# Sliding-window attention as banded matmuls on an even/odd token order, with the row sums as a 29th column of V

## The chip, the cores and the metric

One core of one Trainium2 chip (trn2). The metric is device time in microseconds (us) of one execution; lower is better. A run of a kernel here means several executions, and the median is quoted. Medians are over all executions; ratios are over fast ones alone. Some executions are marked slow: one of four in qk_twice, rz_merge and cap4_merge_flex, two of six in cap4_flex_zg. All other runs quoted are in the fast state.

Engines are named as the profile names them: PE (TensorE matmuls), PEld (its weight loads), DVE (VectorE), ACT (ScalarE), POOL (GpSimd), SP (the queue that issues DMAs). PEclk is the TensorE clock that was granted, as a share of full speed.

## The reference, cut to what matters

One transformer block on 2048 tokens of width 448: a sliding-window attention (A) and a token-shift MLP (B), with residuals.

```python
def _A_ref(x, wqkv, wo):                # H = 16 heads of 28, W = 8, dil = 2
    q, k, v = split(x @ wqkv)
    idx = pos[:, None] - off[None, :]   # off = 0, 2, 4, ..., 14: eight keys per query
    logits = einsum("bhsd,bhswd->bhsw", q, k[idx]) * 28 ** -0.5   # masked where idx < 0
    o = einsum("bhsw,bhswd->bhsd", softmax(logits), v[idx])
    return o @ wo
def _B_ref(x, w1, w2, w3, w4):
    h = gelu(layernorm(x) @ w1)         # then four column groups shifted by +1, -1, +2, -2 tokens
    x1 = x + shifted(h) @ w2
    return x1 + gelu(layernorm(x1) @ w3) @ w4
h = x + _A_ref(layernorm(x), ...)
out = h + _B_ref(layernorm(h), ...)
```

Each query reads only eight keys, all of its own parity (even or odd token).

## The kernel before

The program is written as a list of operations with a small list scheduler that orders each engine's instructions. Tokens go in four tiles of 512. The attention of one tile, shortened:

```python
# A2: products q*k for all eight offsets on DVE, summed over the head dimension by PE
for c in range(4):
    dve("tensor_tensor", out=ring(slot), in0=q_broadcast, in1=k_shifted, op=mult)   # 112 x 4096
for c in range(4):
    for a8 in range(8):
        mm(L, zc[:, c, 7 - a8 : 7 - a8 + 128], ring(slot)[:, a8*512:(a8+1)*512])     # indicator weights
# softmax over w: DVE max, subtract; ACT exp; DVE sum, reciprocal, multiply
dma(Pd, pb)                       # probabilities to DRAM ...
dma(ring(slot), Pd, broadcast)    # ... and back, copied to the 28 partitions of each head
# A3: products p*v on DVE, summed over the window by identity matmuls on PE
for c in range(4):
    dve("tensor_tensor", out=r4, in0=r4, in1=v_shifted, op=mult)                     # 112 x 4096
for c in range(4):
    for w in range(8):
        mm(ps[0:112, b, :], ident[0:112, 0:112], r4[:, :, w, :], w == 0, w == 7)
    act(actT, ps, Copy)
# then WO, with a further identity matmul that adds the residual xin
```

LayerNorm takes its inverse square root by three Newton steps on DVE, and its normalization runs on ACT. PSUM banks are handed out in a fixed rotation.

## Time and profile before

306.95 us (306.94 to 307.39, three executions).

| | us |
|---|---|
| span of the profiled execution | 306.6 |
| PE busy | 260.6 (85%) |
| DVE busy | 168.8 (55%) |
| ACT busy | 154.7 (50%) |
| PE not busy (306.6 - 260.6) | 46.0 |

From the page of before, parts 1 and 2: first busy time, share of the span and instructions of each engine; then the span in 40 equal slices, each digit the busy share in tenths.

```profile
PE 260.6 (85%) x1297; PEld 136.4 (44%) x1297; DVE 168.8 (55%) x346; ACT 154.7 (50%) x240; POOL 19.7 (6%) x44
...
PE   0499959959995799996777988949899999989996
...
DVE  3659889983799728985762789001801640200221
...
PEclk9999979979999599998999999986999999999999
```

The left half (attention) has both PE and DVE full and empty in turn; the right half (MLP) is PE, with little else. The same by stretches, cut at 144 us (columns: stretch, its length, busy time of PE, PEld, DVE, ACT, POOL with instruction counts, granted clock, DMA share, GB/s):

```profile
0.00:144.00 144.00, 115.18 (x530) 62.37 (x531) 109.46 (x183) 65.09 (x102) 3.58 (x28) 0.95 0.53 126
144.00:306.60 162.60, 145.41 (x768) 74.07 (x766) 59.32 (x164) 89.57 (x138) 16.08 (x16) 0.97 0.16 41
```

Much of the PE work on the left is arithmetic that a matmul of q with k would not need. Groups of instructions by shape (the line L630 is a helper's that issues everything, so groups are told apart by their names: name of output and inputs, stationary and moving shape, count | busy us in total, mean ns of one | idle time before them and who ended it):

```profile
L630 DVE TENSOR_TENSOR arena<-arena 112x4096 bf16<-112x4096 bf16 x32 | 72.0, 2287 | 17.6 <-PE ps L630 9.5 <-DMA arena<-attn_p_scratch 7.5 <-ACT arena L630 0.3
L630 PE MATMUL ps<-actT,arena 112*112 112x512 bf16 x192 | 51.0, 432 | 13.3 <-ACT actT L630 12.7 <-DVE arena L630 0.7
L630 PE MATMUL ps<-arena,ident 112*112 112x512 bf16 x128 | 28.8, 380 | 0.8 <-DVE arena L630 0.8
L630 PE MATMUL ps<-arena,zc 112*128 112x512 bf16 x128 | 28.3, 380 | 0.0
```

These are the two rounds of DVE products, QKV, the identity matmuls that sum over the window, and the indicator matmuls that sum over the head dimension. The chain of waits (start us, length us, what) shows how they alternate for one tile:

```profile
101.60 14.55 PE ps L630 x56
116.18 13.30 DVE arena L630 x6
```

### The profile page before, as it was taken

To read this page: it belongs to the slowest core of one execution; us is meant where nothing else is said; L and a number is where in the kernel's file an instruction comes from. 1 tells how busy PE (TensorE), PEld (TensorE's weight loads), DVE (VectorE), ACT (ScalarE), POOL (GpSimd) and SP (SyncE) were. 2 spreads that over 40 slices of the span, in tenths; PEclk is the share of its full clock that TensorE was granted. 3 is DMA by queue.
4 is the path that set the end of the run, shared out by engine and by line. 5 is a ranking of instruction groups with operands and counts; after the bars stand their busy time and mean duration, and the time that the engine had idled before them with its cause. 6 is when DMAs were issued, how large, how long until landed. Compare 5 with 4: busy or idle time off the path is not lost.

```text
span 306.6 us, 3389 instructions
## 1 busy us (share of the span) xinstructions
PE 260.6 (85%) x1297; PEld 136.4 (44%) x1297; DVE 168.8 (55%) x346; ACT 154.7 (50%) x240; POOL 19.7 (6%) x44
## 2 busy tenths in 40 slices
PE   0499959959995799996777988949899999989996
PEld 0254435526542365452444554425445544544552
DVE  3659889983799728985762789001801640200221
ACT  1522346446730567524897568695663167066000
POOL 4000000000000000000000005002205002300000
PEclk9999979979999599998999999986999999999999
DMA  7900018837850299915885000000000100100111
GB/s 224 327 4 0 3 32 202 197 84 175 195 112 0 63 200 207 205 33 145 196 178 191 0 0 2 0 1 0 2 0 30 33 0 0 47 15 0 32 45 45
DMA packets 11824, 24.71 MB, mean 81 GB/s; under 512 B 1376, under 2 KB 9120, under 8 KB 10016
## 3 DMA queue, kind: packets, MB, share of 16 engines
q1 hardware_dynamic: 11808, 24.50, 32.6%
q8 instruction: 10, 0.16, 0.2%
q14 instruction: 6, 0.05, 0.1%
HBM read 22.13 MB, written 2.36 MB: 80 GB/s over the span
## 4 chain that ended last, share of the span: by engine, by line
PE 53%; DVE 27%; ACT 15%; issue 3%; DMA 1%
PE ps L630 53%; DVE arena L630 17%; ACT actT L630 7%; ACT lntm L630 4%; ACT arena L630 3%; DVE st L630 3%; DVE rs_t L630 1%; DVE rs_y L630 1%; DMA xin<-in_A_x_dram 1%; DVE mv L630 1%; DVE ls L630 1%; ACT ls L630 1%; DVE mx L630 1%; ACT L630 0%; DVE rs_x L630 0%
## 5 line engine op out<-in xcount | busy, mean ns | idle before, releaser
L630 PE MATMUL ps<-actT,arena 112*128 112x512 bf16 (+1 forms) x416 | 100.8, 404 | 17.2 <-ACT actT L630 16.6
L630 ACT ACTIVATE arena<-ps 112x512 bf16<-112x512 f32 (+1 forms) x114 | 68.0, 597 | 46.4 <-PE ps L630 46.3
L630 DVE TENSOR_TENSOR arena<-arena 112x4096 bf16<-112x4096 bf16 x32 | 72.0, 2287 | 17.6 <-PE ps L630 9.5
L630 PEld LDWEIGHTS ps<-actT,arena 112*128 112x128 bf16 (+1 forms) x416 | 48.7, 121 | 66.7 <-ACT actT L630 22.2
L630 ACT ACTIVATE actT<-ps 112x1024 bf16<-112x1024 bf16 (+1 forms) x40 | 32.6, 846 | 29.5 <-PE ps L630 29.5
L630 DVE TENSOR_TENSOR ost<-ps,arena 128x448 bf16<-128x448 f32 x16 | 10.0, 625 | 64.6 <-PE ps L630 64.6
L630 PE MATMUL ps<-arena 128*128 128x448 bf16 x224 | 42.9, 353 | 0.0
L630 ACT ACTIVATE lntm<-xin,nbias,rs_y 128x448 bf16<-128x448 bf16 x32 | 22.9, 750 | 17.6 <-DVE nbias L630 17.6
L630 PEld LDWEIGHTS ps<-arena 128*128 128x128 bf16 x224 | 21.9, 98 | 20.7
L630 PE MATMUL ps<-arena,ident 112*112 112x512 bf16 x128 | 28.8, 380 | 0.8 <-DVE arena L630 0.8
L630 PE MATMUL ps<-arena,zc 112*128 112x512 bf16 x128 | 28.3, 380 | 0.0
L630 DVE BATCH_NORM_STATS2 st<-xin 128x6 f32<-128x448 bf16 x32 | 19.3, 604 | 15.6 <-ACT xin L630 11.0
L630 PE MATMUL ps<-ident,lntm 128*112 128x128 bf16 x192 | 15.5, 229 | 13.9 <-ACT lntm L630 13.8
L630 POOL TENSOR_TENSOR arena<-arena,xin 128x448 f32<-128x448 f32 x16 | 16.1, 1035 | 110.8 <-ACT lntm L630 110.8
L630 PE MATMUL ps<-wo_s,actT 112*128 112x448 bf16 x64 | 17.2, 379 | 6.7 <-ACT actT L630 6.4
L630 PE MATMUL ps<-actT,w_s 112*112 112x512 bf16 x64 | 18.6, 441 | 4.6 <-ACT actT L630 4.6
L630 PEld LDWEIGHTS ps<-arena,ident 112*112 112x112 bf16 x128 | 16.5, 130 | 11.9 <-DVE arena L630 1.3
L630 PEld LDWEIGHTS ps<-ident,lntm 128*112 128x112 bf16 x192 | 14.0, 136 | 17.2 <-ACT lntm L630 15.0
L630 DVE TENSOR_TENSOR arena<-ps,arena 128x448 f32<-128x448 f32 x16 | 9.6, 599 | 21.7 <-PE ps L630 21.6
L630 PEld LDWEIGHTS ps<-arena,zc 112*128 112x128 bf16 x128 | 12.4, 98 | 15.0 <-issue 0.2
L630 ACT ACTIVATE ls<-ls 128x512 f32<-128x512 f32 x4 | 2.5, 630 | 28.4 <-DVE ls L630 28.4
L630 PEld LDWEIGHTS ps<-actT,w_s 112*112 112x112 bf16 x64 | 9.0, 150 | 12.2 <-ACT actT L630 6.6
(39 smaller groups left out, 134.4 us busy)
## 6 DMA issues: line engine op xcount, KB each, us to landing
arena<-attn_p_scratch SPq DMA_DIRECT2D x64, 224.0 KB
arena<-in_B_w_dram SPq DMA_DIRECT2D x2, 1568.0 KB, 11.5
xin<-in_A_x_dram SPq DMA_DIRECT2D x4, 448.0 KB, 8.2
out_dram<-ost SPq DMA_DIRECT2D x16, 112.0 KB, 1.7
arena<-in_A_wqkv_dram SPq DMA_DIRECT2D x1, 1176.0 KB, 7.4
w_s<-in_B_w_dram SPq DMA_DIRECT2D x2, 392.0 KB, 8.8
attn_p_scratch<-pb SPq DMA_DIRECT2D x4, 128.0 KB, 1.8
wo_s<-in_A_wo_dram SPq DMA_DIRECT2D x1, 392.0 KB, 10.3
```

Of the source, the lines that this page charges most:

```text
L630: inst = getattr(eng, op.meth)(**op.kw)
```

## The change

The intent is to let PE do both products. Tokens are kept in even and odd halves, so the eight keys of a query are eight neighbours, and 103 queries of one parity need 110 consecutive keys. One matmul of 110 keys by 103 queries (28 deep) then makes a whole band block for a head; exp runs on ACT without a maximum, a 0/1 mask on DVE cuts the block to its band, and a second matmul multiplies by V. V has a 29th column that is constant, so its product is the row sum times that constant. The row sums lie in one partition per head and are packed by DMA over 128 partitions for the reciprocal, stored, and broadcast back.

```diff
+    BLK = [(103 * b, 103, 103 * b + 1) for b in range(4)] + [(412, 100, 410)]   # query start, count, key start
+    KB = 110
@@ attention of one tile (t = token half and parity)
+        for c in range(4):                       # four heads per c
+            for jp in range(2):
+                T = tile(2)                      # two PSUM banks
+                for q0, nq, k0 in BLK:
+                    for j in (2 * jp, 2 * jp + 1):
+                        mm(T[0:KB, j % 2, q0:q0 + nq], kT[32*j:32*j+28, par, c, k0:k0 + KB],
+                           qT[32*j:32*j+28, par, c, q0:q0 + nq], True, True)
+                act(pj, T, ACT.Exp, 1024, scale=SCALE)
+                dve("tensor_tensor", 1024, out=pj, in0=pj, in1=m_, op=ALU.mult)
+            T = tile()
+            for blk, (q0, nq, _) in enumerate(BLK):
+                for j in range(4):
+                    mm(T[32*j:32*j+32, 0, q0:q0 + nq], vt[0:KB, par, blk, 4*c + j, :], pt[0:KB, sl, j, q0:q0 + nq], True, True)
+            copy(osb[:, par, c, :], T)
+        for j in range(4):
+            dma(zp[32*j:32*j+32, par, :], osb[32*j+28:32*j+29, par, :, :])       # pack the row sums
+        dve("reciprocal", out=rzp[:, par, :], in_=zp[:, par, :])
+        dma(zd, rzp[:, par, :])
+        for j in range(4):
+            dma(rzb[32*j:32*j+32], bass.AP(rz_d, (4*t + j) * 2048, [[0, 32], [1, 2048]]))   # broadcast
+        for c in range(4):
+            dve("tensor_tensor", out=oT[:, par, c, :], in0=osb[:, par, c, :], in1=rzb[:, c, :], op=ALU.mult)
... (cuts: loads, LayerNorm, MLP phases)
@@ LayerNorm: power on POOL, normalization on DVE (ACT before)
+        S.add("pool", "tensor_tensor", ..., in0=vtmp, in1=mhalf, op=ALU.pow)
+        S.add("dve", "tensor_scalar", 390, ..., op0=ALU.subtract, op1=ALU.mult)
@@ WO: the residual is added by DVE from PSUM, no identity matmul
+            dve("scalar_tensor_tensor", ..., in0=T, scalar=DOWN, in1=xin, op0=ALU.mult, op1=ALU.add)
@@ scheduler: PSUM banks chosen while ordering; a copy may go to ACT or DVE; shorter look-ahead
+        for b in range(0, 8, n): ...             # place(n): first free run of n banks
@@ end: exp without a maximum can overflow, so the old program stays as a second path
+                        emit_fast(e, eng)
+                        eng.wait_ge(flag_op.sem, flag_op.val)
+                            eng.reg_load(reg, flag[0:1, 0:1])
+                            with eng.If_ne(reg, 0):
+                                emit_general(e, eng)
```

## The prediction

> **What bounds the kernel now.** The page's busy table gives PE 260.6 of 306.6 us, DVE 168.8, ACT 154.7. Split at 144 us (busy by stretches): attention holds 115 us of PE and 109 us of DVE work in 144 us; the MLP part holds 145 us of PE in 163 us and is PE-bound. Attention alternates: in the chain of waits, DVE products (13.3 us for six 4096-wide multiplies, twice), then max/subtract/exp, then PE bursts of 54 to 56 matmuls. Much of that PE work is overhead: groups by shape show 28.3 us of 128 matmuls that sum products over the head dimension, 28.8 us of 128 identity matmuls that sum over the window, 6.1 us of 16 identity matmuls for the residual.
>
> **Removed.** PE: 28.3 + 28.8 + 6.1 = 63 us. DVE: 32 multiplies at 2287 ns (72 us), max/subtract/sum/divide (about 12 us), the Newton chains (about 25 us, now a power on POOL). ACT: 64 normalizations (45 us, now on DVE), the residual copy (8.5 us). 3.6 MB of broadcast DMA per 512 tokens becomes 1 MB.
>
> **Added.** PE: 640 attention matmuls of about 103 columns. The nearest thing in the trace is a transpose of 128 columns: 16 run in 1.05 us, weight loads hidden, about 55 ns each apart from the first. Estimate 45 to 50 ns, so about 30 us. The Trainium skill (TensorE: Matmul & The Clock Gate, Part 3) says that matmuls in different 32-row groups run concurrently, which could make it 22; TensorEngine Tiling (Key Properties) says that changing the tiling mode drains the array, which costs some back. No run shows either yet. QKV: 128 matmuls with 128 weight columns at 222 ns instead of 266, plus 80 of 448 columns: 45 us against 51.
> ACT: 32 exponentials of 110x1024, about 1.02 us each by the 1024-wide copy, 33 us. DVE: 32 mask multiplies near 0.65 us (21 us), 16 output scalings at 0.69 us (11 us), 64 normalizations near 0.35 us. Copies out of PSUM go to ACT or DVE.
> Row sums: gather, reciprocal, store, broadcast: three DMA legs near 2 us, about 10 us of latency per tile, hidden where other tiles' matmuls fill it.
>
> **Sum.** PE: 260.6 - 63 - 6 + 30 = about 221 us. In attention ACT and DVE hold about 72 us each against 92 of PE, so PE bounds it if the order overlaps well. PE idle: 12 until the first dense matmul (now 14.9; the padded weight copy waits for the weights); 12 in attention; 6 in the MLP part (17 now); 4 at the end, with the flag test and the branch over the general path; 4 for lower clock. Total 221 + 38 = 259 us.
>
> Predicted 259 us, 8 in 10 between 246 and 274. Faster by over 2%: 0.97; within 2%: 0.02; slower: 0.01.
>
> **What would show it.** PE busy 215 to 230 us and 80% or more of the span; DVE and ACT 110 to 150 each; the 640 small matmuls at 25 to 35 us in the groups; last attention matmuls before 125 us; PE never waiting over 3 us for the reciprocal's broadcast; the last 130 us a near solid PE row.
>
> **What would make it wrong.** Small matmuls at 80 ns or more (weight loads exposed): +20 us. Half clock in attention. Mask multiplies not at the 4096-wide rate: +17 us of DVE. Exp or PSUM banks holding up PE: attention becomes ACT-bound. The last tile's reciprocal chain exposed: +5 to 10. Row groups overlapping fully: about 8 us less.

## The result, and the profile after

251.51 us (249.73 to 252.7, four executions) against 307.06 us in the same rounds: ratio 0.8183, 95% interval 0.8144 to 0.8221. Ratios here are the mean time of fast runs of one kernel over that of the other (in the experiments the profiled execution itself is left out), so they are not quite the quotient of the medians. The predicted 259 (246 to 274) holds the measured time. A second run (after_again, chip 14) gave 252.39 us, ratio 0.8223.

The page after, the same parts:

```profile
PE 224.6 (90%) x1681; PEld 112.9 (45%) x1681; DVE 138.2 (55%) x306; ACT 120.7 (48%) x175; POOL 46.2 (18%) x71
...
PE   0799799999979998898995999899998999899992
...
DVE  7596862595785677877999602700385008700220
...
PEclk9999659999965995589998899999999999999998
```

PE busy falls by 36.0 us (260.6 to 224.6) and PE not busy by 20.0 us (46.0 to 26.0); together that is the whole 56.0 us between the two profiled spans. By stretches, cut at 115 us:

```profile
0.00:115.00 115.00, 99.26 (x1012) 53.07 (x1013) 81.23 (x185) 72.99 (x100) 20.30 (x41) 0.85 0.42 97
115.00:250.60 135.60, 125.35 (x671) 59.83 (x669) 56.94 (x122) 47.68 (x75) 25.90 (x31) 0.98 0.08 22
```

The first stretch is no longer shared between PE and DVE in turn: PE is busy for 99.26 of 115 us. But its clock is 0.85, lower than the 0.95 of before. The groups by shape name what came, and what the clock did:

```profile
L1100 PE MATMUL ps<-hT,arena 112*128 112x512 bf16 x128 | 39.4, 453 | 0.5 <-ACT hT L1100 0.2 <-ACT arena L1100 0.2
L1100 ACT ACTIVATE pt<-ps 110x1024 bf16<-110x1024 f32 x32 | 30.3, 1030 | 7.8 <-PE ps L1100 7.8
L1100 DVE TENSOR_TENSOR pt<-pt,msk 110x1024 bf16<-110x1024 bf16 x32 | 21.0, 684 | 1.7 <-ACT pt L1100 1.7
L1100 PE MATMUL ps<-qT,kT 28*110 28x103 bf16 x256 | 11.8, 232 | 3.8 <-ACT pt L1100 3.5
L1100 PE MATMUL ps<-pt,vt 110*32 110x103 bf16 x256 | 8.0, 253 | 2.0 <-DVE pt L1100 1.4 <-ACT pt L1100 0.7
L1100 PE MATMUL ps<-qT,kT 28*110 28x100 bf16 x64 | 6.5, 220 | 0.0
L1100 PE MATMUL ps<-pt,vt 110*32 110x100 bf16 x64 | 4.3, 253 | 0.0
```

The last four lines are the 640 small matmuls, each kind in two shapes. Their busy times must not be added (11.8 + 8.0 + 6.5 + 4.3 = 30.6 us): the last two matmuls of a burst, of the other shape, run while the earlier ones still do, and the overlap would count twice. The page, which puts the shapes together, has for the scores:

```profile
L1100 PE MATMUL ps<-qT,kT 28*110 28x103 bf16 (+1 forms) x320 | 13.2, 229 | 3.8 <-ACT pt L1100 3.5
```

With 9.1 us for the products with V, put together in the same way, the 640 small matmuls are busy for 22.3 us. The exponentials and the masks cost what the copies and the products of before implied. The surprise is the first line: 128 projections of q and k, which at the 222 ns each of the same shape in before should take 28.4 us, take 39.4 us. The line of before:

```profile
L630 PE MATMUL ps<-actT,arena 112*128 112x512 bf16 x224 | 49.7, 380 | 3.9 <-ACT actT L630 3.9
```

Why, can be seen where the small matmuls run alone. The order of PE in one such place (start us, length us, instruction, count, idle time before it and who ended it):

```profile
66.82 1.24 PE L1100 MATMUL ps<-qT,kT 28*110 28x103 bf16 x40
68.39 0.46 PE L1100 MATMUL ps<-qT,kT 28*110 28x103 bf16 x10 [0.33 <-ACT pt L1100]
69.30 0.46 PE L1100 MATMUL ps<-qT,kT 28*110 28x103 bf16 x10 [0.46 <-ACT pt L1100]
70.22 0.46 PE L1100 MATMUL ps<-qT,kT 28*110 28x103 bf16 x10 [0.46 <-ACT pt L1100]
```

The first 40 are four groups of two banks each: with that all eight PSUM banks hold scores that wait for their exponential. From there PE gets one bank pair back per exponential (one in 0.91 us), fills it with ten matmuls, and waits; no projection can start, as it has no bank (cap4, below, tests this). The ten take 0.46 us, of which the last one's own length is 0.21 us: in the trace's records they start in pairs 3 ns apart, one pair every 51 ns after the first, so the array is fed for only about a quarter of a microsecond in 0.91. The Trainium skill (TensorE: Matmul & The Clock Gate, Part 3) gives about 4 ns between the starts of matmuls in different row groups; 3 ns agrees.

Then the clock falls. Busy time by stretches of 3 us (columns as above; the clock is the third number from the end):

```profile
24.00:27.00 3.00, 1.55 (x40) 1.05 (x34) 2.96 (x9) 3.00 (x5) 0.00 (x0) 0.92 1.05 220
27.00:30.00 3.00, 2.56 (x33) 1.33 (x34) 2.73 (x7) 2.67 (x4) 1.54 (x2) 0.50 1.09 325
30.00:33.00 3.00, 3.00 (x16) 0.97 (x14) 2.39 (x4) 1.01 (x1) 0.61 (x1) 0.50 0.41 133
33.00:36.00 3.00, 3.00 (x45) 1.21 (x45) 0.94 (x2) 1.51 (x2) 0.00 (x0) 0.50 0.02 5
```

ACT is full (3.00 of 3) in the first line, PE half empty. In the following lines PE is nearly or quite full again (2.56, then 3.00 of 3), but it runs at half clock. The trace's clock records put this spell at 26.5 to 36.7 us; there are further ones at 70.9 (10.2 us), 94.8 (13.7 us) and 135.7 (3.4 us), 37.5 us in all before the last store, against 23.9 us in before, though before has 56 us more span. In the records of after, the q and k projections start 426 ns apart (median) at half clock and 216 ns apart at full clock, so up to half of such a spell is lost if PE is full in it.

### The profile page after: what moved, and what is told of

It is laid out like the page before. It is cut to its first block, busy times and chain, and to the rows that moved or that the text cites. A ratio compares the mean times of both kernels' runs of the same rounds, so it can differ in the third digit from the quotient of the medians.

```text
span 250.6 us, 4082 instructions
## 1 busy us (share of the span) xinstructions
PE 224.6 (90%) x1681; PEld 112.9 (45%) x1681; DVE 138.2 (55%) x306; ACT 120.7 (48%) x175; POOL 46.2 (18%) x71
## 4 chain that ended last, share of the span: by engine, by line
PE 72%; DVE 16%; ACT 5%; POOL 2%; issue 2%; DVEq 0%
PE ps L1100 72%; DVE st L1100 4%; DVE lntm L1100 4%; ACT pt L1100 3%; DVE xb L1100 2%; POOL rstd L1100 2%; DVE mv L1100 1%; DVE oT L1100 1%; ACT hT L1100 1%; ACT actT L1100 1%; DVE pt L1100 1%; ACT arena L1100 0%; POOL vtmp L1100 0%; DVE xin L1100 0%; DVE msk L1100 0%
## 5 line engine op out<-in xcount | busy, mean ns | idle before, releaser
L1100 PE MATMUL ps<-actT,w_s 112*128 112x512 bf16 (+1 forms) x288 | 64.2, 382 | 1.2 <-DVE mv L1100 1.1
L1100 ACT ACTIVATE arena<-ps 128x512 bf16<-128x512 f32 (+1 forms) x67 | 40.0, 597 | 28.0 <-PE ps L1100 27.8
L1100 PE MATMUL ps<-w_s,arena 128*128 128x448 bf16 x224 | 43.9, 353 | 0.0
L1100 PEld LDWEIGHTS ps<-actT,w_s 112*128 112x128 bf16 (+1 forms) x288 | 25.9, 106 | 37.8 <-ACT arena L1100 15.2
L1100 PE MATMUL ps<-hT,arena 112*128 112x512 bf16 x128 | 39.4, 453 | 0.5 <-ACT hT L1100 0.2
L1100 ACT ACTIVATE pt<-ps 110x1024 bf16<-110x1024 f32 x32 | 30.3, 1030 | 7.8 <-PE ps L1100 7.8
L1100 PEld LDWEIGHTS ps<-w_s,arena 128*128 128x128 bf16 x224 | 21.5, 98 | 20.5 <-DVE xb L1100 0.6
L1100 DVE TENSOR_TENSOR pt<-pt,msk 110x1024 bf16<-110x1024 bf16 x32 | 21.0, 684 | 1.7 <-ACT pt L1100 1.7
L1100 POOL TENSOR_TENSOR rstd<-vtmp,mhalf 128x4 f32<-128x4 f32 (+1 forms) x19 | 18.5, 972 | 1.6
L1100 POOL TENSOR_TENSOR xb<-xb,xin 128x448 bf16<-128x448 bf16 x16 | 16.7, 1072 | 1.5 <-DVE lntm L1100 1.5
L1100 PE MATMUL ps<-qT,kT 28*110 28x103 bf16 (+1 forms) x320 | 13.2, 229 | 3.8 <-ACT pt L1100 3.5
L1100 ACT ACTIVATE gT<-ps 112x512 bf16<-112x512 f32 x16 | 9.6, 600 | 12.3 <-PE ps L1100 12.3
```

The source lines that it names most:

```text
L1100: inst = getattr(eng, op.meth)(**op.kw)
```

## The experiments

All edits are to the changed kernel unless said otherwise. "after" is the changed kernel; its ratio to before was 0.8183 and 0.8223, 0.820 on average. The theory that the first ones test: attention after the change loses time to the half clock, which comes from score tiles filling PSUM. The main rival: the half clock is a symptom, and PE work, ACT or DVE bound the time.

### The scheduler alone (gen_only)

```diff
-        S, flag_op = _fast_path(...); ...; emit_fast(e, eng); flag test
+        emit_general = _plan(nc, es, _general_path(nc, es, *args), "g_")
```

> The old program (DVE products, identity matmuls) in the order of the new list scheduler, no fast path. Theory: nearly all of the 55 us comes from the new attention and the moved normalizations, so this runs at 295 to 312 us. Rival: the new scheduler itself removed most of the idle time of the MLP part (17 us of PE idle before), so this runs at 285 us or less.

Measured: 307.89 us against 307.63, ratio 0.9998 (0.9958 to 1.0038). That is in the theory's range. The instruction order on PE and ACT does differ from before's, but the time does not. So the new scheduling rule gives nothing to the old program, whose banks and engines are fixed. What it does with free choice of banks and engines in the new program was not tested alone.

### Small matmuls twice (qk_twice, pv_twice)

```diff
                     for j in (2 * jp, 2 * jp + 1):
+                      for _ in range(2):
                         mm(T[...], kT[...], qT[...], True, True)
```

and the same around the product with V.

> Every q-k matmul of the fast path is issued twice into the same place (result unchanged). Theory: inside a burst they start 28 ns apart (ten in 0.46 us including a 0.21 us tail), and PE waits for exponentials there anyway, so 320 more cost 0 to 9 us: 250 to 260 us. Rival: they cost the 57 ns each that the busy table gives (18.3 us for 320): 268 to 271 us.

> Every probability-value matmul is issued twice (result unchanged). Theory: 20 ns each inside a burst (twenty in 0.62 us including the tail), partly in PE wait time: 0 to 6.5 us more, 251 to 258 us. Rival: the busy table's 38 ns each: 263 us.

Measured: 257.61 us (one execution of four slow), ratio 0.8334 (0.8283 to 0.8386), for the scores; 252.05 us, ratio 0.8173 (0.813 to 0.8216), for V. Against 0.820 that is 1.6% or about 4 us for 320 more score matmuls, and nothing visible for 320 more V matmuls. The theory's range holds for both and the rival's for neither.

The rivals' 57 and 38 ns each (18.3 and 12.3 us over 320) were no busy times to begin with, but the double count of above; put together, the groups give 41 and 28 ns (13.2 and 9.1 us over 320). Doubled, they grow to 22.0 and 14.0 us, which is 27 and 15 ns for each matmul added. For V a part of that price is hidden: half clock adds up to 23.9 us in pv_twice, against 37.5 in after and 30.7 in after_again (and 37.6 in qk_twice). All four executions of pv_twice have a higher granted clock (0.947 to 0.953) than any of after (0.920 to 0.934). So that small matmuls are cheap is shown for the scores; for V, "nothing" is their cost less what the clock gave back.

### Room in PSUM (cap4)

```diff
-            for b in range(0, 8, n):
+            for b in range(0, 4 if n > 1 else 8, n):
```

> The q-k result tiles (two PSUM banks each) may only lie in banks 0 to 3, so at most two wait for their exponential and four banks stay free for dense matmuls. Theory: in after, PE runs four q-k groups ahead, fills PSUM, then idles behind the exponentials, and the granted clock falls to 0.50 for about 10 us, three times (34 us in all), which stretches the dense matmuls behind it; with the cap they interleave, the clock stays near 1 in attention, and the time falls to 238 to 247 us. Rival: attention is bound by the exponentials and DVE themselves, and the clock only follows: 250 us or slower.

Measured: 246.8 us (244.22 to 247.31), ratio 0.7998 (0.7945 to 0.8052), correct. That is 2.5% below after's 0.820, and the intervals do not touch: **cap4 beats both kernels**. It lies in the theory's range, near its upper end. It was run at another time. The stretches that were at half clock in after:

```profile
24.00:27.00 3.00, 2.70 (x43) 1.79 (x41) 1.90 (x5) 3.00 (x4) 0.00 (x0) 1.00 1.07 276
27.00:30.00 3.00, 3.00 (x32) 1.26 (x30) 3.00 (x6) 1.92 (x3) 0.00 (x0) 1.00 0.91 282
30.00:33.00 3.00, 2.67 (x73) 1.66 (x74) 2.48 (x5) 2.24 (x4) 0.00 (x0) 1.00 0.04 13
33.00:36.00 3.00, 3.00 (x49) 1.42 (x44) 3.00 (x6) 2.57 (x4) 0.45 (x1) 1.00 0.03 5
```

In the first line ACT is as full as before, but PE has projections to run between the bursts. The clock stays at 1.00 until 87 us; half clock falls from 37.5 to 20.5 us. What is left moved to the seam between attention and MLP (87.0, 104.0 and 124.5 us). One edit changes the order of all engines, so this run alone does not separate the clock from better interleaving; the next one does.

### More work, for the clock's sake (filler)

```diff
                 T = tile(2)
+                for a_ in range(2):
+                    mm(T[:, a_, :], ident[:], msk[:, 0, :], True, True)     # overwritten by the scores
```

> Before each burst of ten q-k matmuls two dense 128x128x512 matmuls write the same two banks, which the burst then overwrites (result unchanged). That is 64 more matmuls, 14 us of PE at full clock, 27 us at half. Theory: the half clock comes from PE's low activity while it waits for exponentials; the fillers keep it busy there, the clock in attention stays above 0.95, and the time changes by -6 to +4 us: 245 to 256 us. Rival: PE work is what counts and the clock is not tied to these waits: 264 us or more.

Measured: 250.38 us, ratio 0.8166 (0.8132 to 0.82), against 0.8223 for after on the same chip; the theory's range held. PE got 64 dense matmuls more (14 us at full clock) and the kernel became no slower. The bursts still come ten at a time and wait for the exponentials (68.7 to 72.7 us in its trace), but the clock is full. The stretch from 12 to 132 us, first in after and then in filler (the clock is the third number from the end):

```profile
12.00:132.00 120.00, 111.41 (x1082) 59.20 (x1080) 88.91 (x194) 75.52 (x106) 14.97 (x24) 0.86 0.35 78
```

```profile
12.00:132.00 120.00, 114.54 (x1153) 60.76 (x1160) 88.20 (x199) 79.86 (x113) 17.86 (x29) 1.00 0.33 78
```

Half clock was left only at 132.2 us (3.4 us) before the last store; the projections' line reads:

```profile
L1102 PE MATMUL ps<-hT,arena 112*128 112x512 bf16 x128 | 31.4, 390 | 0.2
```

31.4 us instead of 39.4: of the 11 us too many in after, 8 go with the clock. The rival (264 us or more) is out: the idle of PE between bursts is what costs the clock. The time is about 2 us below after's although 14 us of fillers were added, of which part ran where PE would have waited. So about 16 us is an upper estimate of the clock's price in after. It agrees with half of the half-clock time that the fillers removed: 17 us against the profile of after, 14 against that of after_again.

### The second path's test at the end (no_general)

```diff
-                        eng.wait_ge(flag_op.sem, flag_op.val)
-                        with eng.register(...): reg_load, If_ne, emit_general
```

> Without the general path, the flag load and the branch (the flag is still computed; right only for inputs without overflow). Theory: the end of the span, 4.2 us after the last vector instruction against 2.2 us in before, shortens by 2 us: ratio to after 0.992. Rival: the store itself is slower and the branch is free: no change.

> The changed kernel once more, for the same chip and rounds as the three others: 249.5 to 253 us.

Measured: 249.17 us, ratio 0.8128 (0.807 to 0.8186), against 252.39 us and 0.8223 (0.8193 to 0.8253) for after_again, which is after itself. The quotient is 0.988, a little more than the 0.992 expected; the intervals just miss each other. In after's trace, the flag's load and branch on SP after the last store take 1.1 us, and the last store itself, from issue to its semaphore, 2.7 us against 1.7 in before. The size is right to within the noise. The longer store belongs to the second path too: the last store takes 1.7 us in no_general, as in before and gen_only, and 2.4 to 3.4 us in every run with the second path. By which way is not shown.

### The reciprocal's way through DRAM (no_rz, no_rz_last)

Both give wrong results: a constant stands for the broadcast reciprocal.

```diff
-        for j in range(4): dma(zp...)   # gather
-        dve("reciprocal", ...); dma(zd, rzp); for j in range(4): dma(rzb...)
```

(no_rz for all tiles; no_rz_last for the last tile only.)

> Wrong on purpose: the gather, reciprocal, store and broadcast of the row sums are dropped and a constant stands in for the broadcast tile. Theory: their latency (about 11 us per tile) is filled by other tiles' matmuls, so the time changes by less than 2 us: 249 to 252 us. Rival: the last tile's chain (att 3 to WO 3) is exposed, PE waits there: 3 to 8 us less, 243 to 248 us.

> Wrong on purpose: only the last of the four tiles drops its row-sum transfers and takes a constant; the first three keep them. Theory: the 10 us that no_rz gained are the last tile's chain, which holds back WO 3, then B1 3, then the first W3 (134.6 us in after, 124.9 in no_rz): this alone gains 8 to 11 us, 241 to 244 us. Rival: the gain is the DMA traffic and the vector work of all four tiles: a quarter of it, 249 us.

Measured: no_rz 241.17 us, ratio 0.7882 (0.7828 to 0.7935), 4.1% or about 10 us below after of the same call. no_rz_last 248.29 us, ratio 0.8116 (0.8057 to 0.8174), 1% or about 3 us below after's 0.820, at the edge of the intervals (0.8223 for after on the same chip). So the theory that the latency is hidden fell, and the rival's 243 to 248 us was too high as well. The next theory, that the last tile's chain alone is the cost, fell too; there the rival's number, a quarter of the gain or 249 us, is close, but its cause, DMA traffic and vector work, is not shown by that. In no_rz the last WO (the output projection, o @ wo) starts at 102.13 us instead of 126.16, and the block of matmuls with w1 of the last tile and w3 of the first starts at 127.78 us instead of 138.14, which is the whole gain. First the line of that block in after, then in no_rz (the end of the view's window cuts both):

```profile
138.14 2.18 PE L1100 MATMUL ps<-actT,w_s 112*112 112x512 bf16 x7
```

```profile
127.78 12.55 PE L1091 MATMUL ps<-actT,w_s 112*112 112x512 bf16 x57 [0.60 <-DVE actT L1091]
```

In no_rz_last, WO of the last tile is also early (106.38 us), but w1 of the last tile starts only at 133.01 us, about 5 us earlier than in after. In between, PE waits three times for DVE or ACT and runs at half clock:

```profile
123.29 0.54 PE L1103 MATMUL ps<-ident,lntm 128*112 128x128 bf16 x6 [1.08 <-DVE xb L1103]
124.45 0.77 PE L1103 MATMUL ps<-ident,lntm 128*112 128x128 bf16 x10 [0.62 <-DVE lntm L1103]
125.88 5.38 PE L1103 MATMUL ps<-actT,w_s 112*112 112x512 bf16 x16 [0.67 <-ACT actT L1103]
```

Sixteen matmuls in 5.38 us, against 3.65 us for the sixteen of the next tile at 133.01. The half clock totals 20.5 us in no_rz, and 30.7 in both no_rz_last and after_again. By this, up to about 5 us of no_rz's 10 us (half of 10.3) may be the clock again. How the rest divides between the four chains, and the changed order of DVE at the seam, stays open.

### Fewer, larger DMAs (rz_merge), and with everything else (cap4_merge_flex)

```diff
-        for j in range(4): dma(zp[32*j:32*j+32], osb[32*j+28:32*j+29])
+        dma(zp[:, par, :], osb[28:128:32, par])
-        for j in range(4): dma(rzb[32*j:32*j+32], AP(rz_d, ..., [[0, 32], [1, 2048]]), bytes=32 * 8192)
+        dma(rzb[:], AP(rz_d, 4*t*2048, [[2048, 4], [0, 32], [1, 2048]]), bytes=128 * 4096)   # told half the bytes
```

cap4_merge_flex adds cap4's edit and lets three of the four kinds of normalization go to ACT or DVE.

> Result unchanged: per tile one gather instead of four and one broadcast instead of four, and the scheduler is told half the bytes for the broadcast, so that it does not plan the scaling later than the data. Theory: seven issues of 0.4 to 0.6 us less in the chain and about 4 us of scaling behind other vector work go away: the last chain shortens by 4 to 7 us and the time falls by 3 to 6 us, to 246 to 249 us. Rival: one large broadcast lands no earlier than four, and PE finds other work: 251 us or more.

> A candidate for the better version: q-k tiles in banks 0 to 3, merged row-sum transfers, and the LN normalizations of three of the four places may go to ACT or DVE. Theory: the clock (5 us in cap4), the last chain (3 to 6 us) and vector work at the seam of attention and MLP (DVE over 2.7 of 3 us from 84 to 126 us in cap4) add up: 236 to 242 us. Rival: they all pay in the same stretch, and only the largest counts: 245 us.

Measured: 297.5 us, ratio 0.9673 (0.9619 to 0.9727), and 292.34 us, ratio 0.9501 (0.9449 to 0.9554), both correct. The edit of rz_merge cost about 45 us. Both theories failed; rz_merge's rival gave "251 us or more", but for a reason (the broadcast lands no earlier and PE finds other work) that did not hold either. (One execution of four of each, the profiled one, is slow; the fast ones, 296.11 to 298.76 and 290.65 to 293.42 us, and the ratios say the same.) The waits of DVE in rz_merge (who waited for whom: total us, times, longest):

```profile
DVE oT L1099 <- DMA rzb<-rz_scratch: 45.5, 4, 14.0
```

45.5 us of DVE standing still for the broadcast, once per tile. The masks of the next tile come later in DVE's list and stand behind it, and PE behind them: before the products with V, PE waited 28.9 us for masks in rz_merge, against 1.4 us in after. The stretch of one such broadcast in rz_merge, then the stretch of the last tile's four broadcasts in after (the DMA share is the last number but one):

```profile
51.00:68.00 17.00, 9.53 (x129) 4.33 (x129) 5.88 (x10) 8.56 (x12) 0.67 (x1) 0.86 0.22 63
```

```profile
113.60:119.50 5.90, 5.21 (x25) 2.73 (x26) 4.54 (x14) 3.04 (x5) 2.50 (x4) 1.00 0.81 178
```

The merged transfer uses 0.22 of the 16 DMA engines, which is 3.5 of them, at 63 GB/s for about 17 us; four separate ones use 0.81 at 178 GB/s and land a median 4.4 us after issue. The Trainium skill (DMA: Bandwidth & Descriptors, "How many engines (k)") says that the slowest dimension of size above one decides over how many engines a transfer is spread: over the largest number up to 16 that divides it on both sides. The merged pattern begins with 4 on the DRAM side, the separate ones with 32. The measured 3.5 fits 4, and 0.81 of 16, or 13, is near the 16 of the separate ones. The scheduler, which had been told half the bytes, would then place the scaling early in DVE's list, which turns latency into a stop; this is argued, as no run has the merge without the changed size. Which share is the spread and which the too optimistic plan was not separated.

### Last candidate (cap4_flex_zg)

cap4, normalizations to ACT or DVE, the gather merged, the broadcasts separate.

> Last candidate: q-k tiles in banks 0 to 3, normalizations to ACT or DVE, and only the gather of the row sums merged (one transfer of 32 KB, seen to land within 2.3 us of its issue); the four broadcasts stay separate. Theory: cap4's gain (about 5 us against after) stays, three issues less per chain take 1 to 2 us off, and moving normalizations off DVE at the seam gives 1 to 4 us: 240 to 245 us. Rival: the seam is bound by the chain of dependent steps, not by DVE's load, and an ACT normalization is twice as long (0.75 against 0.39 us): 246 to 249 us.

Measured: 247.39 us (245.74 to 250.26, six executions; the four fast ones 245.74 to 248.99), ratio 0.803 (0.7987 to 0.8073): not to be told from cap4 (0.7998). Half clock fell further, to 10.2 us, and still nothing clear was gained. In the seam, 84 to 126 us, first cap4 and then this kernel:

```profile
84.00:126.00 42.00, 35.46 (x259) 17.87 (x258) 35.29 (x81) 15.71 (x21) 6.17 (x10) 0.78 0.23 50
```

```profile
84.00:126.00 42.00, 35.93 (x302) 20.11 (x302) 34.95 (x77) 30.52 (x44) 11.52 (x21) 0.92 0.25 53
```

ACT took on 15 us more, the clock rose from 0.78 to 0.92, and PE is still busy for only 36 of 42 us, with DVE at 35 as before. Lower load on DVE was thus not reached, and a better clock there was not enough. The rival's reading, that dependent steps bind in the seam, fits, but is not shown: no run shortens such a step, and none shows which it is.

## Why the prediction was right, and where not

- **Time: right, in part by errors that cancel.** 251.51 us lies in 246 to 274; the centre of 259 was 7.5 us too high. The profiled span of 250.6 us differs from 259 by four terms of the prediction's sum: small matmuls 22.3 instead of 30 (-7.7), the rest of PE's busy time 202.3 instead of 221 - 30 = 191 (+11.3), idle without the clock 26.0 instead of 34 (-8.0), and the 4 for the clock, which are not idle time (-4).
- **PE busy: right in size, by luck in part.** 221 predicted, 224.6 measured, 90% of the span; DVE 138.2 and ACT 120.7 lie in the 110 to 150 that the prediction gave. But the sum is right because small matmuls that were put too high stand against a clock that was put too low. The removal of about 63 us of PE work and the interleaving of what is left fit the gain (36.0 us less busy, 20.0 us less idle). Only the scheduler was run alone: how the gain divides between the new attention, the moved LayerNorm work and the residual is argued, not shown.
- **Small matmuls: too high.** 22.3 us of busy time, below the 25 to 35 that was to show the prediction right, and what it gave for the case that row groups overlap ("could make it 22"). One does not take 45 to 50 ns: at full clock the matmuls of a score burst start 27 ns apart on average and those of a V burst 11 ns; the rest is about 0.2 us of tail behind a burst, and slower bursts at half clock. qk_twice shows it for the scores: 320 more cost about 4 us.
- **Clock: the term that was mis-sized.** "4 for lower clock" should have been up to about 16 by filler. It hides in the busy time, in the +11.3 us of above: the q and k projections took 39.4 us instead of the 28.4 that the prediction's own 222 ns gives. It was offset by idle time and small matmuls that were put too high. The prediction had named "half clock in attention" as a risk, without a size.
- **Idle: too high.** 12 + 12 + 6 + 4 = 34 us without the clock, against 26.0. The first projection started at 10.4 us, and PE idled 8.1 us before 11.56; the MLP stretch has 10.2 us not busy (135.60 - 125.35) including the end, and attention between 11.56 and 115 us only 7.7.
- **Row sums "hidden where other tiles' matmuls fill it": wrong.** The waits of PE on the broadcast are indeed short (0.3 us in all, 0.5 us at most for a weight load), as the prediction asked. But no_rz is 10 us faster. PE filled the wait with later work, then ran out of it at the seam. A short direct wait did not prove that the latency was free. The prediction had named an exposed last chain as a risk of 5 to 10 us; no_rz_last shows about 3 us for that tile alone.
- **Mask multiplies: right**, 684 ns each against 650 predicted, 21.0 us.
- **Last attention matmul before 125 us: right**, at 105 us.

## What to carry to other kernels

When tiles that wait for a slow engine can fill all of PSUM (here four of two banks each), cap how many of them may exist, so that dense matmuls still find a bank: here one such line was worth 2.5%, by clock and interleaving. Read the granted clock beside the busy table; a busy PE at half clock looks like work. Do not add the busy times of groups whose instructions overlap. A DMA chain that no engine is seen to wait for is tested by removing it, not by the wait table; and before merging DMAs, look at the outermost dimension of the merged pattern.

## What the Trainium skill lacked or had wrong

- TensorE: Matmul & The Clock Gate ("Why this matters for your kernels") asks for no PE idle gap over about 3 us to keep the clock. Here the clock halved at 26.5 and 70.9 us although no idle gap in the preceding 3 us was over 0.5 us; bursts that fed the array about a quarter of a microsecond in every 0.91 were enough. The page does say, under "A second HAM failure mode: psum-queue depth-cycling", that frequent short idles between groups of matmuls make the clock swing, as here; it lacks a length or a share of activity at which they do.
- The same page (Part 1) says that the clock returns after at least one busy window of about 3.4 us. Here spells before the last store lasted 3.4 to 23.9 us (3.4, 6.8, 10.2 or 13.7 us in after and before), all near multiples of 3.4, which agrees with a window of that size. In after, PE was busy without a break from 30 us and the clock returned only at 36.7.
- The same page ("Back-to-back issue gap") gives about 25 ns as the least distance between starts. The distance of overlapping row tiles in this trace is 3 ns, as its own Part 3 has it (about 4); the average over a burst at full clock was 27 ns for the scores, and 11 ns for the products with V, below that figure.
- TensorEngine Tiling (Key Properties) says that a change of tiling mode drains the array. The page gives no time for it. No run here isolates one; the records show something that can hold it. At full clock a dense matmul with 512 columns is followed by the next one 216 ns after its start, but by a small one 309 ns after (median in filler), and the next dense one starts 140 ns after the last small one, where two score pairs are 51 ns apart. Whether that is a drain or a weight load is open.
- DMA: Bandwidth & Descriptors ("How many engines (k)") fits what was seen: 0.22 of 16 engines, or 3.5, for a pattern that begins with 4.
